# Blocks 0 and 1 of a gated linear attention in front of two MoE layers: the fourth head pair placed by products instead of a shift

## The chip, the cores and the metric

One core of a Trainium2 chip runs the whole program in one launch. The metric is the device time of one execution in microseconds (us); lower is better. The engines are PE (TensorE, matmuls), DVE (VectorE), ACT (ScalarE), POOL (GpSimd) and SP (SyncE, which issues the DMAs). Each engine works through its own instructions in order, and semaphores order the engines among each other.

## The reference

```python
# q, k, v, alpha: [4 batches, 8 heads, 768 steps, 48]
for t in range(S):
    state = alpha[:, :, t, :, None] * state + einsum('bhd,bhe->bhde', k[:, :, t], v[:, :, t])
    y[:, :, t] = einsum('bhd,bhde->bhe', q[:, :, t], state)
x = y.transpose(0, 2, 1, 3).reshape(3072, 384)          # heads side by side
x = ((x @ w_a) * (x @ w_b)) @ w_out                      # 384 -> 1536 -> 384
h = x @ w_in                                             # 384 -> 2048 -> 384
out = (max(h, 0) + alpha2 * min(h, 0)) @ w_out2
```

## The kernel before, in words

The 3072 tokens are cut into 24 chunks of 128 (one batch each) and 6 blocks of four chunks (512 tokens); `n` is the block, `c` the chunk in it. A chunk's 8 heads lie as 4 pairs: `j` is the pair, `i` the half of the partitions (rows 0 to 47 and 64 to 111), and each head fills 48 of 64 rows. MoE matmuls run in FP32R with every operand split into a high and a low part, three matmuls for each product (lines 699, 700 and 702). The weights arrive as 64-bit floats; `conv` makes high and low parts of them, one unit (128 x 768) in six to eight operations on DVE and ACT, with the low part on PE for the units a0, b0 and o0 (`ON_PE`, lines 308 to 310, tile `cl`). Of a0 and b0, `conv` does the first and the second 384 columns one after the other (`halves`), so that the first half of the output columns is ready early.

**The planner.** The program's order is written out by a small list scheduler, `Graph`. Every operation is added with its engine, an estimated duration in ns, a key, the operations that it waits for and sometimes a ring or pool of buffers. The scheduler walks through estimated time and gives each engine, whenever it is free, the ready operation with the smallest key. Where it leaves PE without work for more than 500 ns, `fill` (line 185, tile `wp`) puts bf16 matmuls of ones there, for 0.7 of the gap. On the chip the order is fixed and only the semaphores decide when something runs.

**The steps of the first MoE.** `SEGMENTS` lists them: four steps of block 0 with the units 0 and 1, four of block 1 with the same units, then both blocks with the units 2 and 3, and so on. A step is one tile of 128 hidden columns: an `up` with `a` and one with `b` (9 matmuls each into a PSUM bank of two, `ps_mm`), the product on DVE, its split (ACT, DVE), and two steps later a `down` of 9 matmuls. The ups are chained (`up_before`), so no step of block 1 comes ahead of block 0's four, and none of block 0's unit 2 ahead of block 1's four.

**A chunk.** `scan_r`, `recip`, `scan_a` and `mul` on DVE (lines 402 to 417) scale k and q by running products of alpha. PE transposes k (`kps`, line 453), ACT copies it (`ks`). `pe_a` makes the products of k and q, DVE masks them (`As`). Then

- blocks 1 to 5 work in halves of 64 steps, with tiles of 64 x 64: `pe_a` at line 481, `pe_cross` (`intra` at line 558 for one half of each head, the two states at line 581), `mid` (the state z1 in the middle, DVE), `pe_own` (the other `intra`, then `inter` at line 565 with Z for the first half and z1 for the second). `A` and `y` share one pair of PSUM banks (`pring`), so a chunk's `pe_a` waits until the chunk before has left `y`.
- block 0 has no state before it and works in whole chunks: `pe_a` at line 471, the state at line 528, `pe_y` at lines 544 and 548.

`y` holds four tiles of heads, and the first MoE reads three (`KT`), with 16 free rows (`GR`) beside each head's 48. The two heads of the fourth tile go into these gaps. In block 0 this is done by products with `vg`, a second layout of v that comes from memory with zeros in place (line 548). In block 1 (`moved`), ACT copies the fourth tile out (`ev_3`) and three matmuls with shifted identities add it to the other three (`pe_m`, line 611). In blocks 2 to 5, DMAs move it. `split_h` (ACT, line 657) and `split_l` (DVE, line 661) make the high and low part `x` that the MoE reads.

```python
for h, z in ((0, Z[:, c]), (1, s["z1"])):          # the end of pe_own before
    for j in range(NJ):
        for i in range(2):
            inter(j, i, h, z, h == 1 and j > 1)
```

Of the kernel before, what the change touches and what calls it, by code (L numbers as in the profile page):

```python
# [11 lines left out]
F32 = mybir.dt.float32  # L12
BF16 = mybir.dt.bfloat16
F32R = mybir.dt.float32r
# [7 lines left out]
P = 128  # L22
# [117 lines left out]
def body(tc, akq, v, vg, w_a, w_b, w_o1, w_in, w_o2, beta, out):  # L140
# [13 lines left out]
    with ExitStack() as ctx:  # L154
# [12 lines left out]
        mask = const.tile([P, P], F32, name="mask")  # L167
# [10 lines left out]
        def fill(t0, t1):  # L178
# [13 lines left out]
        nc.gpsimd.affine_select(  # L192
            out=mask, in_=mask, pattern=[[1, P]], compare_op=ALU.is_ge, fill=0.0,
            base=0, channel_multiplier=-1,
        )
# [4 lines left out]
        shift = gpool.tile([P, KT + 1, P], F32, name="shift", tag="x2")  # L200
        nc.gpsimd.memset(shift, 0.0)
        for t in range(KT):
            for i in range(2):
                nc.gpsimd.tensor_copy(
                    out=shift[:, t, 64 * i + D : 64 * i + 64],
                    in_=eye[:, 64 * i + GR * t : 64 * i + GR * (t + 1)],
                )
# [16 lines left out]
        def conv(src, tag, name, key, wait, sink, early=15000, on_pe=False, halves=None):  # L224

            b = {}
            tags = (halves[0], tag) if halves else (tag, tag)
            nt = halves[1] if halves else 1  # L230

            def load():
                b["raw"] = wpool.tile([P, UC], I64, name=f"r{name}", tag=tags[0])
                nc.sync.dma_start(b["raw"], src)

            ld = G.add("SP", 2100, load, key - early, wait, 4000)
            free = cring.take()
            last, highs = [], []
            for n in range(2 if halves else 1):
                N = 2 if halves else 1  # L240
                part = lambda x, n=n: x.rearrange("p (t n f) -> p t n f", t=nt, n=N)[:, :, n, :]
                word = lambda k, dt, part=part: part(b["raw"].bitcast(dt)[:, k::2])
                c1 = lambda part=part: part(b["c1"])
                c2 = lambda part=part: part(b["c2"])
                hi = lambda part=part: part(b["r"][:, 0:UC])
                lo = lambda part=part: part(b["r"][:, UC : 2 * UC])

                def magnitude(n=n, c1=c1, word=word):
                    if n == 0:
                        b["c1"] = cpool.tile([P, UC], F32, name="c1", tag="c1")  # L250
                        b["c2"] = cpool.tile([P, UC], F32, name="c2", tag="c2")


                    nc.scalar.activation(out=c1(), in_=word(1, F32), func=ACTF.Abs, scale=2.0**-112)

                def sign(c2=c2, word=word):
                    nc.vector.tensor_scalar(out=c2().bitcast(U32), in0=word(1, U32),
                                            scalar1=0x80000000, scalar2=None, op0=ALU.bitwise_and)

                def main(c1=c1, c2=c2):  # L260
                    x = c1().bitcast(U32)
                    nc.vector.scalar_tensor_tensor(out=x, in0=x, scalar=3, in1=c2().bitcast(U32),
                                                   op0=ALU.logical_shift_left, op1=ALU.bitwise_or)

                def power(c1=c1, c2=c2):
                    nc.vector.tensor_scalar(out=c2().bitcast(U32), in0=c1().bitcast(U32),
                                            scalar1=0xFF800000, scalar2=None, op0=ALU.bitwise_and)

                def rest(c2=c2, word=word):
                    o = c2()  # L270
                    nc.vector.scalar_tensor_tensor(out=o, in0=word(0, U32), scalar=2.0**-52,
                                                   in1=c2(), op0=ALU.mult, op1=ALU.mult)

                def high(n=n, c1=c1, hi=hi):
                    if n == 0:
                        b["r"] = wpool.tile([P, 2 * UC], F32R, name=f"w{name}", tag=tag)
                    nc.scalar.copy(hi(), c1())

                def sub(c1=c1, hi=hi):
                    nc.vector.tensor_tensor(out=c1(), in0=c1(), in1=hi().bitcast(F32), op=ALU.subtract)  # L280

                def low(c1=c1, c2=c2, lo=lo):
                    nc.vector.tensor_tensor(out=lo(), in0=c1(), in1=c2(), op=ALU.add)
                    sink(b["r"])

                d = lambda t: t // N + 40
                m = G.add("ACT", d(910), magnitude, key, [ld, *(free if n == 0 else ())], after=last)
                x = G.add("DVE", d(550), sign, key, [m])
                x = G.add("DVE", d(930), main, key, [x])
                x = G.add("DVE", d(550), power, key, [x])  # L290
                x = G.add("DVE", d(930), rest, key, [x])
                x = G.add("ACT", d(830), high, key, [x], after=highs)
# [729 lines left out]
```

## Time and profile before

| | |
|---|---|
| median of 3 runs (lowest, highest) | 967.24 us (966.16, 967.24) |
| the profiled execution: its own time, its span | 966.85 us, 965.2 us |
| PE, busy share of the span | 99% |
| DVE, ACT | 62%, 26% |
| filler matmuls `wp`, line 185 | 125, in the first tenth of the span |
| mean granted TensorE clock | 0.999 |

The span runs from the first to the last instruction; 1.65 us of the execution's time lie around it. A busy PE is not PE at its peak: matmuls overlap, and a row of the timeline gives start and length of a run of them, where the length includes the last one's way through the array, so that the distance to the next row's start is what the run costs. In these rows a float32 product counts as two instructions (16 for 8 products of the code).

### The profile page before, as it was taken

The numbers are of one execution on the slowest core, as the hardware profiler recorded it, in microseconds if no ns is written. First come the engines' busy times: TensorE is split into PE (matmuls) and PEld (weight loads), VectorE is DVE, ScalarE is ACT, GpSimd is POOL, SyncE is SP. The second block draws the span as 40 slices with busy tenths as digits, with TensorE's granted clock in tenths as the row PEclk, the third lists the DMA queues.
The fourth block names the chain that finished last, engine by engine and source line by source line (L and its number), as shares of the span: only waits on it lengthen the run. The fifth ranks groups of instructions, "written<-read, shape, count | busy, mean of one in ns | idle before, by whom it ended". The sixth has DMA issues, their size and how long they took to land.

```text
span 965.2 us, 15549 instructions
## 1 busy us (share of the span) xinstructions
PE 952.7 (99%) x6667; PEld 770.4 (80%) x6667; DVE 600.4 (62%) x887; ACT 253.9 (26%) x422; POOL 4.4 (0%) x18
## 2 busy tenths in 40 slices
PE   6999999999999999999999999999999999999998
PEld 5778888778877887887788888888888888888886
DVE  7999888578668868865332254555555545545554
ACT  2444443233333333332221211111111111111111
POOL 1000000000000000000000000000000000000000
PEclk9999999999999999999999999999999999999999
DMA  8971000145456545742065550010100200200000
GB/s 317 407 287 51 12 1 12 45 145 180 150 179 204 206 167 191 240 153 79 25 210 197 196 196 1 27 72 1 65 33 1 89 10 0 99 1 1 33 1 33
DMA packets 31076, 104.09 MB, mean 108 GB/s; under 512 B 3488, under 2 KB 4256, under 8 KB 31008
## 3 DMA queue, kind: packets, MB, share of 16 engines
q1 hardware_dynamic: 30864, 102.97, 30.2%
q8 instruction: 52, 0.85, 0.4%
q10 hardware_dynamic: 144, 0.13, 0.0%
q14 instruction: 16, 0.13, 0.0%
HBM read 74.78 MB, written 26.74 MB: 105 GB/s over the span
## 4 chain that ended last, share of the span: by engine, by line
PE 99%; DVE 0%; DMA 0%; ACT 0%; issue 0%; DVEq 0%; ACTq 0%
PE acc L699 12%; PE acc L702 12%; PE acc L700 12%; PE pi L699 7%; PE pi L702 7%; PE pi L700 7%; PE pb L699 5%; PE pa L699 5%; PE pa L700 5%; PE pb L700 5%; PE pb L702 5%; PE pa L702 5%; PE wp L185 2%; PE y L558 2%; PE kps L453 1%; PE A L481 1%
## 5 line engine op out<-in xcount | busy, mean ns | idle before, releaser
L722 ACT CAST gh<-ng 128x512 fp32r<-128x512 f32 x96 | 59.6, 621 | 328.6 <-DVE ng L935 275.0
L931 DVE TENSOR_SCALAR ng<-pi,betaT 128x512 f32<-128x512 f32 x96 | 72.1, 751 | 106.7 <-PE pi L702 105.8
L726 DVE TENSOR_TENSOR gl<-ng,gh 128x512 fp32r<-128x512 f32 x96 | 66.3, 691 | 79.9 <-ACT gh L722 79.9
L699 PE MATMUL pi<-x,v 128*128 128x512 f32 x288 | 113.3, 393 | 0.0
L700 PE MATMUL acc<-gh,v 128*128 128x512 f32 x288 | 113.1, 393 | 0.0
L702 PE MATMUL acc<-gl,v 128*128 128x512 f32 x288 | 112.9, 392 | 0.0
L700 PE MATMUL pi<-x,v 128*128 128x512 f32 x288 | 112.7, 391 | 0.0
L699 PE MATMUL acc<-gh,v 128*128 128x512 f32 x288 | 112.1, 389 | 0.0
L829 DVE TENSOR_TENSOR a_sb<-a_sb,pb 128x512 f32<-128x512 f32 x72 | 49.4, 686 | 96.5 <-PE pb L702 96.4
L699 PE MATMUL pa<-x,wa 128*128 128x512 f32 x216 | 86.7, 401 | 0.0
L699 PE MATMUL pb<-x,wb 128*128 128x512 f32 x216 | 86.6, 401 | 0.0
L699 PE MATMUL acc<-gh,wo 128*128 128x512 f32 x216 | 86.6, 401 | 0.0
L702 PE MATMUL acc<-gl,wo 128*128 128x512 f32 x216 | 84.9, 393 | 0.0
L700 PE MATMUL pa<-x,wa 128*128 128x512 f32 x216 | 84.7, 392 | 0.0
L700 PE MATMUL pb<-x,wb 128*128 128x512 f32 x216 | 84.6, 392 | 0.0
L700 PE MATMUL acc<-gh,wo 128*128 128x512 f32 x216 | 84.6, 392 | 0.0
L826 ACT COPY a_sb<-pa 128x512 f32<-128x512 f32 x72 | 42.2, 587 | 151.0 <-PE pa L702 151.0
L702 PE MATMUL pi<-x,v 128*128 128x512 f32 x288 | 81.5, 391 | 0.0
L722 ACT CAST gh<-a_sb 128x512 fp32r<-128x512 f32 x72 | 44.8, 622 | 102.6 <-DVE a_sb L829 102.6
L935 DVE SCALAR_TENSOR_TENSOR ng<-pi,ng 128x512 f32<-128x512 f32 x96 | 66.4, 691 | 3.1
L699 PEld LDWEIGHTS pi<-x,v 128*128 128x128 f32 x288 | 54.1, 188 | 13.7 <-DVE ng L935 2.1
L699 PEld LDWEIGHTS acc<-gh,v 128*128 128x128 f32 x288 | 54.0, 188 | 12.3
(120 smaller groups left out, 1426.5 us busy)
## 6 DMA issues: line engine op xcount, KB each, us to landing
kq<-in_akq SPq DMA_DIRECT2D x24, 512.0 KB, 3.8
w2d<-ws SPq DMA_DIRECT2D x16, 768.0 KB, 3.5
v<-w2d SPq DMA_DIRECT2D x16, 768.0 KB, 5.4
x2d<-x SPq DMA_DIRECT2D x18, 512.0 KB, 3.3
x<-x2d SPq DMA_DIRECT2D x6, 1536.0 KB, 6.9
ra<-in_akq SPq DMA_DIRECT2D x24, 258.5 KB, 3.5
v<-in_v SPq DMA_DIRECT2D x24, 256.0 KB, 4.4
rs<-in_w_in SPq DMA_DIRECT2D x8, 768.0 KB, 5.5
```

The costliest lines, as they stand in the source:

```text
L185: nc.tensor.matmul(wp, warm[:, 0:P], warm, start=True, stop=True)
L453: nc.tensor.transpose(s["kps"][:, j, :], kT()[:, j, :], ident)
L558: nc.tensor.matmul(y_of(k, half(p), part_of(h)), s["v"][part_of(h), 2 * j + i, :], s["As"][part_of(h), i, j, :], start=first, stop=False, ...
L699: nc.tensor.matmul(o, lh, rh, start=first and n == 0, stop=False)
L700: nc.tensor.matmul(o, ll, rh, start=False, stop=False)
L702: nc.tensor.matmul(o, lh, rl, start=False, stop=last and n == len(pairs) - 1)
L722: nc.scalar.copy(gq[idx][0], src())
L726: nc.vector.tensor_tensor(out=gl, in0=src(), in1=gh.bitcast(F32), op=ALU.subtract)
L826: nc.scalar.copy(b["a"], ba["t"])
L829: nc.vector.tensor_tensor(out=b["a"], in0=b["a"], in1=bb["t"], op=ALU.mult)
L931: nc.vector.tensor_scalar(out=b["n"], in0=bh["t"], scalar1=0.0, scalar2=betaT[:, i : i + 1], op0=ALU.min, op1=ALU.mult)
L935: nc.vector.scalar_tensor_tensor(out=b["n"], in0=bh["t"], scalar=0.0, in1=b["n"], op0=ALU.max, op1=ALU.add)
```

## The change

It touches blocks 0 and 1, the planner's keys, and two orders inside `pe_cross` and `pe_own` of all blocks.

1. `vg`, its loads, the shifted identities, `ev_3` and `pe_m` go. A zeroed tile `gaps` is kept, and ACT spreads into its 16-column gaps the fourth pair's v (`gather_v`), the middle state z1 and, in block 1, Z (`gather_z`). PE multiplies with these: `intra_moved` in `pe_cross` and `pe_own`, and `pe_pair` after `pe_own`. `intra` and `inter` leave the fourth tile's heads out in blocks 0 and 1.
2. Block 0 takes the path in halves: `pe_a` with 64 x 64 tiles, one masking operation instead of two, z1 by a copy on ACT, the second state inside `pe_own`. Odd and even chunks have their own `ks`, `As` and PSUM banks. For chunks 0 to 2 the low part of `x` is made by PE (`less`) and copied by ACT (`ev_l`) instead of subtracted on DVE.
3. a0 and b0 are converted whole, with a key of -50000 that puts their load and their operations behind block 0 and ahead of block 1. The estimate for the low part on PE falls from 1600 to 1000 ns.
4. In the first segment an `up` is issued as three pieces of three matmuls and a `down` as three pieces.
5. The keys of block 1's chunks lie 8000 apart instead of 9500 and begin earlier; masking, z1 and the splits of block 1 go ahead of everything but block 0 (`chain_early`). The chunks of blocks 2 to 5 get earlier keys too.
6. In all blocks `pe_own` takes the z1 products of `i = 0` first, then its `intra`, then the z1 products of `i = 1`, then those with Z. `pe_cross` goes through the states with the halves of the chunk outside and `i` inside.

```diff
-        shift = gpool.tile([P, KT + 1, P], F32, name="shift", tag="x2")
...
+        gaps = wpool.tile([P, 4, KT, 2, 64], F32, name="gaps", tag=f"w{3 * NU1 - 1}")
+        other = wpool.tile([P, 2 * UC], F32, name="other", tag=f"w{3 * NU1 - 2}")
+        nc.gpsimd.memset(gaps, 0.0)
...
+                                   due[x] - 18000 if u or nm == "o" else -50000, (), sink,
+                                   on_pe=x in ON_PE)
...
-            key = block_at[n] - (BC - c) * 9500 - 6000 if n else c * 1000 - 100000
+            key = block_at[n] - (BC - c) * 12000 - 14000
+            if first:
+                key = c * 1000 - 100000 if start else block_at[1] - (BC - c) * 8000 - 16000
+            odd = start and c % 2
+            chain_early = 100000 if n == 1 else 0
...
+            def intra_moved(k, h):
+                for p in range(2):
+                    nc.tensor.matmul(y_of(k, half(p), part_of(h)), gaps[part_of(h), c % 2, k, p, :],
+                                     s["As"][part_of(h), 1, 2 + p, :], start=False, stop=False,
+                                     skip_group_check=True)
...
+            def state_of(h, j):
+                for i in range(2):
+                    nc.tensor.matmul(dS_of(h)[half(i), j // 2, j % 2, :], s["ks"][part_of(h), j, half(i)],
+                                     s["v"][part_of(h), 2 * j + i, 0:D], start=False, ...
+            def pe_cross():
...
+                for j in range(NJ):
+                    for h in range(2):
+                        intra(j, 1 - h, h, j < 2)
+                if first:
+                    for k in range(KT):
+                        intra_moved(k, 1 - k // 2)
+                for j in range(NJ):
+                    state_of(0, j)
+                    if not (start or end):
+                        state_of(1, j)
...
+            def pe_own():
+                for j in range(NJ):
+                    inter(j, 0, 1, False)
+                for j in range(NJ):
+                    for i in range(2):
+                        intra(j, i, i, False)
+                if first:
+                    for k in range(KT):
+                        intra_moved(k, k // 2)
+                for j in range(NJ):
+                    inter(j, 1, 1, j > 1)
+                if start:
+                    for j in range(NJ):
+                        state_of(1, j)
+                    return
+                for j in range(NJ):
+                    for i in range(2):
+                        inter(j, i, 0, j > 1)
+            def spread(to, src):
+                nc.scalar.copy(to[:, :, :, D:], src.rearrange("p j (t r) -> p t j r", r=GR))
...
+            def pe_pair():
+                for h in range(1 if start else 0, 2):
+                    for k in range(KT):
+                        for p in range(2):
+                            nc.tensor.matmul(y_of(k, half(p), part_of(h)), gaps[:, 2 + h, k, p, :],
+                                             qT()[:, 2 + p, part_of(h)], start=False, stop=True, ...
+            def less():
+                for x, y in two(0):
+                    nc.tensor.matmul(y, minus, x, start=False, stop=True, skip_group_check=True)
+            def ev_l():
+                for x, y in two(1):
+                    nc.scalar.copy(x, y)
...
-            if moved:
-                def ev_3(): ...
-                def pe_m(): ...
```

## Rows read from the trace of the kernel before

**Rows 1.** The page: the chain that ended last, by engine.
```profile
PE 99%; DVE 0%; DMA 0%; ACT 0%; issue 0%; DVEq 0%; ACTq 0%
```

**Rows 2.** Filler of line 185 by stretch: PE busy (x), weight loads, clock, DMA share, GB/s.
```profile
8.00:35.00 27.00, 7.04 (x47) 5.01 (x47) 1.00 0.98 372
35.00:90.00 55.00, 10.06 (x78) 7.03 (x78) 1.00 0.65 247
```

**Rows 3.** All engines: PE, PEld, DVE, ACT, POOL busy, clock, DMA share, GB/s.
```profile
8.00:35.00 27.00, 27.00 (x317) 21.91 (x321) 26.05 (x44) 9.40 (x25) 0.00 (x0) 1.00 0.98 372
```

**Rows 4.** PE's timeline, block 0's last chunk to the first ups: start, length, work.
```profile
26.03 0.88 PE L544 MATMUL y<-As,v 128*64 128x128 f32 x12
...
29.18 0.91 PE L308 MATMUL cl<-c,plus 128*128 128x384 f32 x2
...
35.35 0.51 PE L699 MATMUL pa<-x,wa 128*128 128x512 f32 x1
...
39.61 0.81 PE L308 MATMUL cl<-c,plus 128*128 128x384 f32 x2
...
41.17 0.46 PE L558 MATMUL y<-As,v 64*64 64x64 f32 x16
```

**Rows 5.** PE's timeline, block 1's last chunk to the first step of block 1.
```profile
75.65 0.60 PE L453 MATMUL kps<-plus,kq 128*128 128x128 f32 x4
...
76.80 0.50 PE L699 MATMUL pb<-x,wb 128*128 128x512 f32 x1
...
81.13 0.46 PE L558 MATMUL y<-As,v 64*64 64x64 f32 x16
81.42 0.63 PE L581 MATMUL y<-v,ks 64*64 64x48 f32 x32
81.98 0.61 PE L185 MATMUL wp<-ones 128*128 128x256 bf16 x4
...
84.60 0.46 PE L558 MATMUL y<-As,v 64*64 64x64 f32 x16
84.88 0.41 PE L565 MATMUL y<-kq,Z 48*48 48x64 f32 x16
85.11 0.40 PE L565 MATMUL y<-kq,As 48*48 48x64 f32 x16
85.44 1.38 PE L185 MATMUL wp<-ones 128*128 128x256 bf16 x11
86.66 0.83 PE L611 MATMUL y<-shift 128*128 128x128 f32 x6
87.33 2.13 PE L185 MATMUL wp<-ones 128*128 128x256 bf16 x18
89.21 0.48 PE L699 MATMUL pa<-x,wa 128*128 128x512 f32 x1
```

**Rows 6.** DVE by line and shape up to 90 us: count, busy us, mean ns.
```profile
L262 DVE SCALAR_TENSOR_TENSOR c<-c,c 128x768 uint32<-128x768 uint32 x6 | 5.6, 950 | 0.0
L492 DVE TENSOR_TENSOR As<-A,mask 128x512 f32<-128x512 f32 x8 | 5.5, 682 | 0.7 <-PE A L471 0.7
L266 DVE TENSOR_SCALAR c<-c 128x768 uint32<-128x768 uint32 x6 | 3.2, 552 | 0.0
```

**Rows 7.** DVE's timeline: the scans of block 0's first and second chunk, a split.
```profile
3.78 1.26 DVE L402 TENSOR_TENSOR_SCAN ra<-ra,ones 128x516 f32<-128x516 f32 x1 [3.78 <-DMA ra<-in_akq]
...
7.77 1.23 DVE L402 TENSOR_TENSOR_SCAN ra<-ra,ones 128x516 f32<-128x516 f32 x1
...
28.24 0.60 DVE L661 TENSOR_TENSOR x<-y,x 128x256 fp32r<-128x256 f32 x2
```

**Rows 8.** ACT by line and shape up to 90 us.
```profile
L607 ACT COPY shift<-y 128x128 f32<-128x128 f32 x4 | 1.1, 274 | 1.7 <-PE y L565 1.7
```

**Rows 9.** PE's timeline, the states of a chunk of block 5, one half only.
```profile
452.34 0.63 PE L581 MATMUL y<-v,ks 64*64 64x48 f32 x16
452.90 0.50 PE L699 MATMUL pa<-x,wa 128*128 128x512 f32 x1
```

More of the change, by code (lines that the diff above doesn't have):

```diff
@@ new lines, in high, with sub, low @@
+            def high():
+                b["r"] = wpool.tile([P, 2 * UC], F32R, name=f"w{name}", tag=tag)
+                nc.scalar.copy(hi(), b["c1"])
+            def sub():
+                nc.vector.tensor_tensor(out=b["c1"], in0=b["c1"], in1=hi().bitcast(F32), op=ALU.subtract)
+            def low():
+                nc.vector.tensor_tensor(out=lo(), in0=b["c1"], in1=b["c2"], op=ALU.add)
+                sink(b["r"])
+            ld = G.add("SP", 2100, load, key - early, wait, 4000)
+            x = G.add("ACT", 950, magnitude, key, [ld, *cring.take()])
@@ L397, in chunk @@
             lq = A("SP", 1400, load_kq, lwait, 13800, 3000, [la])
-            lv = A("SP", 1250 if start else 720, load_v, vring.take(), 12000, 3000)
+            vwait, vhold = (vring.take(), vring.last()) if spare is None else ([lq], lhold)
+            lv = A("SP", 720, load_v, vwait, 12000, 3000)
             def scan_r():
@@ new lines, in chunk @@
+            if start:
+                (b0, w0, h0), (b1, w1, h1) = (bank(0), bank(KT)) if c % 2 else (bank(1), bank(2))
+                ybanks, w = (b0, b1), [*w0, *w1]
+            else:
+                w, h0, h1 = pring.take(), pring.last(), []
+            gv = A("ACT", 220, gather_v, [lv, *vgring.take()]) if first else None
+            pc = A("PE", 850, pe_cross, [a0, ks, lv, gv, *w])
+            kring.use(pc)
+            z1 = A("ACT" if start else "DVE", 360, mid, [pc, zs], chain_early)
@@ new lines, in chunk @@
+            own = py = A("PE", 850, pe_own, [z1, zs, q1])
+            kring.use(py)
+            if first:
+                gw = gring1.take()
+                x = [A("ACT", 220, lambda: gather_z(1), [z1, *gw])]
+                if not start:
+                    x.append(A("ACT", 220, lambda: gather_z(0), [zs, *gw]))
+                py = A("PE", 500, pe_pair, [own, *x])
+                gring1.use(py)
+                vgring.use(own)
+                o5 = loads[3 * NU1 - 1]
+                py.users.append(o5)
+                o5.need += 1
@@ L746, in down, with f @@
                     wait += accfree.pop()
-            op = G.add("PE", 9 * MM, f, key, [*deps, *wait],
-                       after=[chain.get(acc)])
+            op = None
+            for part in ([[e] for e in range(KT)] if fine else [range(KT)]):
+                def f(part=part):
+                    if first and 0 in part:
+                        accs[acc] = [ps_acc.tile([P, MB], F32, name=f"acc{e}", tag=f"acc{e}")
+                                     for e in range(KT)]
+                    wh, wl = units[w]
+                    g = gq[idx]
+                    for e in part:
+                        es = slice(e * P, (e + 1) * P)
+                        mms(accs[acc][e], products([((wh[:, o, es], wl[:, o, es]), g)]), range(3), first, last)
+                op = G.add("PE", 3 * len(part) * MM, f, key, () if op else [*deps, *wait],
+                           after=[op or chain.get(acc)])
             chain[acc] = op
```

470 lines of the change are left out of this document (194 added, 276 removed).

## The prediction, made before the changed kernel ran

> **What bounds the kernel now.** I read the page first, then the chain of waits, then PE's timeline of the first 90 us beside DVE's. The chain is PE for 99% of the span [rows 1], and from 8 us on PE has no gap [rows 3], so a microsecond of PE work, real or filler, is a microsecond of the span. The filler tells where PE had nothing real to do: 47 matmuls before 35 us, 78 between 35 and 90, which are all 125 that the table of the page counts [rows 2]. Their lengths sum to 17.1 us; a run's length reaches over the next row's start (1.38 us against 1.22 in rows 5), so I take 15 us of the span as filler. The last run ends where the first step of block 1 starts, at 89.2 us [rows 5]. From there on the span is 876 us of nothing but work.
>
> So two questions decide. How much earlier than 89.2 us can block 1's first step start? And does PE get more to do after it? Before it, PE does 89.2 - 8.0 - 15 = 66.2 us of real work.
>
> **What sets the start.** Until 35 us it is DVE: 26.05 us busy of 27 [rows 3]. Afterwards it is a chain: `A` and `y` share one pair of banks, so block 1's chunks follow each other, and the last takes from 75.65 to 89.21, 13.6 us, in which its own PE work is short and PE fills with filler [rows 5].
>
> **The change, part by part.**
>
> *DVE in block 0.* A chunk's four operations take 7.77 - 3.78 = 4.0 us [rows 7], four chunks 16.0. Masking falls from two operations of 0.68 to one [rows 6]: 4 x 0.68 = 2.7 stay. Three low parts of x at 0.6 [rows 7] go to PE and ACT. a0 and b0, whole, are two operations of 0.95 and two of 0.55 each [rows 6]: 6.0 us for both. From 3.8 us on that is 24.7 us, so DVE is through at 28.5. Then come a high part on ACT, which I set at 0.8 us by the DVE operations of the same shape [rows 6], and four low parts on PE at 41.17 - 39.61 = 1.56 us [rows 4], 6.2 us, of which the first two can start while b0 is still on DVE: the first up at about 34.5 us, against 35.35 [rows 4]. That is little earlier, but all four low parts are then done; before, two of the four (3.1 us) came after the first up.
>
> *PE in block 0.* Before, a chunk is 29.18 - 26.03 = 3.15 us [rows 4] and about 0.5 for the transposes. For the new one I need the price of 64 x 64 products. Where consecutive products change between the two row halves, 8 `intra` take 0.29 us, 16 states 0.56, 8 `inter` 0.23 [rows 5]: 0.03 to 0.035 each. Where all lie in one row half, 8 states take as long as 16 did, 0.56 us [rows 9]: twice the price. By these: transposes and `pe_a` as in block 1, 1.15; `pe_cross` with 4 `intra` in turn and 2 in one half (0.28), `intra_moved` with four in one half and two beside them (0.28), 8 states in one half (0.56), 1.12; `pe_own` with 4 + 2 `inter` in one half (0.34), `intra` and `intra_moved` again 0.56, 8 states 0.56, 1.46; `pe_pair` 6 products of 128 rows and 64 columns, for which 6 of double the moving columns give at most 0.88 [rows 4], 0.4; `less` 0.17, by nine matmuls of 512 columns in 2.1 us [rows 4]. Sum 4.3, so +0.65 a chunk, +2.6 for four, and 0.5 for one more change of shape a chunk (0.1 each, below): 3.1 us.
>
> *PE in block 1.* Before: 1.15 + 0.85 + 0.84 + 0.67 (`pe_m`) = 3.5 us a chunk [rows 5]. New: 1.15; `pe_cross` 0.28 + 0.28 + 0.56 = 1.12; `pe_own` 0.34 + 0.56 + 0.22 = 1.12; `pe_pair` 12 products, 0.8 (bounds: 0.4, by the price of a small product, and 1.8, by 0.88 for six). Sum 4.2: +0.7, for four chunks 2.8 us. The copy of 0.27 on ACT [rows 8] becomes three: `pe_cross` now waits for `gather_v`, `pe_pair` for `gather_z`, where `pe_m` waited for `ev_3`. Behind a waiting one on PE stand MoE pieces and all else; `gather_v` needs only v, which lies there early, so I take 0; uncovered, it is 4 x 0.27 = 1.1 us.
>
> *The start of block 1's steps.* By real work alone: 8.0 + 66.2 + 3.1 + 2.8 = 80.1 us. From the other end: first up 34.5, eight ups and four downs at 2.13 (two take 39.61 - 35.35 [rows 4]) 25.6, block 1 without what runs before the first up 15.6, o0's two low parts 3.1: 78.8. Filler on top: a1, b1 and o0 each need 3.0 us of DVE, a1 and b1 two operations of 0.95 more [rows 6], and DVE has first two chunks of block 1 and the products of two steps to do, so PE runs dry once around 45 us; and the planner now sets the low part on PE at 1.0 us where it takes 1.56, so some filler will stand where none is needed. I take 3 us (bounds 0 and 9, what lies between 80.1 and 89.2). Start at 82.5, so 6.7 us are gained. The pieces of three, the earlier keys and the places ahead of the rest are what lets the chunk's chain run in under 13 us; by themselves they add no work on PE. Pieces can change how often PE goes from one shape to another; a change costs 0.1 us (8 `inter` take 0.33 us before filler, 0.23 before more `inter` [rows 5]): ten more would be 1.0 us, inside the 3.
>
> *Blocks 2 to 5.* Here only the order changes. In `pe_own`, 4 products in the lower row half now stand ahead, and 4 in the upper one behind, where before the halves took turns. Eight products at 0.058 instead of 0.029: +0.23 us a chunk, 16 chunks, **+3.7 us** on an engine without a gap. Bounds: nothing, if PE starts the other half's products past a waiting one; 0.28 (by rows 9's states), 4.5 us. The states in `pe_cross` go by pairs of one half; four in a row still use all four tiles, so I take 0; at rows 9's price throughout it would be 0.56 x 12 = 6.7. `pe_own` also begins with z1 now, so that nothing of it hides a late `mid`: at most one operation of 0.7 us on DVE a chunk, but a planned one, so 0.
>
> [...]
>
> *What is hidden.* ACT gets per chunk of block 0 some 1.3 us more (9.4 of 27 us busy [rows 3]); it has room, and the links are in the chain above. POOL clears a larger tile at the start and loses six small copies: it is done before the first `gather_v`. SP loses four loads of `vg`, and the later chunks of block 0 keep v in slots of their own, so that their loads wait for nothing; the DMA engines are 0.98 busy until 35 us [rows 3], so a0 and b0 ahead of the rest delay the others by their 1.5 MB at 372 GB/s, 4 us, which are due only after 28 us. The slots of `gaps` and `other` are freed later, so o5's and b5's loads wait on SP, with the later loads queued behind; they are first used in the fifth segment, so 0. Earlier keys of blocks 2 to 5: no filler stands there that they could remove.
>
> **Sum**, against the profiled execution (966.85 us, span 965.2): -6.7 + 3.7 = -3.0, so a span of 962.2 and a time of 963.9 us. That execution stands 0.4 us below the median shown.
>
> **Rivals.**
> - *The row halves fill each other.* If PE works past a run in one half, the 3.7 us fall away: 960.2 us. For it: four tiles do work at once in rows 5. Against it: rows 9. [...] 18%.
> - *PE never runs dry* after the first up: start at 79.5, 9.7 gained, 3.7 lost: 960.9. Against it: DVE's 26 of 27 us. 10%.
> - *The chunk's chain keeps its pace (slower).* The new chunk has `pe_pair` and its copy in place of `pe_m` and its copy, as many links, and more PE work. If it still takes 13.6 us [rows 5], four from 34.5 end at 88.9: 0.3 gained, 3.7 lost, 970.3 us. It decides from 12.8 us a chunk (start at 85.5), where gain and loss are equal. For it: the in-order queues have as many hops as before. Against it: the pieces of 0.7 instead of 2.1 us and the first places. 18%.
> - *They cancel*: start at 84.5 to 86, or the states by pairs cost a part of their bound: 966 to 968. 18%. This includes that the change gives DVE time which PE's new work takes back.
>
> **The numbers.** The forecast has 36%, its own range is 961.5 to 966.3. A measurement of this kernel tells 0.2%, 1.9 us, from no change. Faster: most of the forecast (0.29), the first two rivals (0.28): 0.57. Same: the rest of the forecast and the cancelling: 0.25. Slower: 0.18. The range of 8 in 10 reaches from 957.5 (both faster rivals in part together) to 970.5.
>
> **What would show it.** First step of block 1 at 82.5 us; filler down from 17 us to about 6; the first up near 34.5 with all four low parts ahead of it. `pe_own` in blocks 2 to 5 at 0.93 us instead of 0.70 up to its last product: if it stays, the first rival holds. `pe_pair` at 0.8 us in block 1. The forecast is wrong if filler stays above 10 us, or if work other than these terms appears after block 1's first step.

## The result, and the profile after

The changed kernel takes 975.98 us (975.34 to 976.51), the one before 966.7: 1.0096 times as long, 95% interval 1.0079 to 1.0114. Forecast were 963.9 us, so 3 us less; it is 9.3 us more, and above the prediction's range of 8 in 10, which ends at 970.5. The profiled execution of the changed kernel took 976.24 us, its span is 974.5. Sums of PE work below are taken from one product's start to the next one's, since lengths overlap (a run of 0.92 us from 90.51 on reaches past the next start at 91.36).

The end of block 1, on PE's timeline of the changed kernel (start, length, line, work), answers to [rows 5]:

```profile
90.51 0.92 PE L579 MATMUL y<-kq,gaps 128*64 128x64 f32 x24
91.36 0.83 PE L185 MATMUL wp<-ones 128*128 128x256 bf16 x6
...
94.11 2.22 PE L702 MATMUL pa<-x,wa 128*128 128x512 f32 x9
```

Block 1's first step starts at 94.11, and one of four downs of the first segment (2.1 us), which all stood ahead of it before, is still to do. Counted with it the step stands at 96.2: 7.0 us later than 89.21, not 6.7 earlier. (In other runs up to two of the four downs are still to do there; the text says where their 2.1 us each are added.) The other 2.4 us come from blocks 2 to 5, where the products `inter` (line 506) take 12.28 instead of 8.94 us and `intra` (line 490) 8.04 instead of 9.01.

Most of the loss is made before the first up. PE's timeline of the changed kernel there answers to [rows 4]:

```profile
14.13 0.66 PE L437 MATMUL kps<-plus,kq 128*128 128x128 f32 x4
...
19.94 0.98 PE L515 MATMUL y<-v,other 64*64 64x48 f32 x14 [1.63 <-issue]
...
23.81 1.11 PE L437 MATMUL kps<-plus,in 128*128 128x128 f32 x4
...
30.17 0.66 PE L437 MATMUL kps<-plus,in 128*128 128x128 f32 x4
...
34.52 0.49 PE L658 MATMUL y<-x,minus 128*128 128x256 f32 x2
...
44.68 2.31 PE L702 MATMUL pa<-x,wa 128*128 128x512 f32 x9
```

Three things are to be seen. Up to 19.94 PE does nothing for 1.63 us, and the bracket names no semaphore but "issue". From then to about 30 us the same work takes 1.7 times as long: four transposes 1.11 instead of 0.66 us. And the first up starts at 44.68 instead of 35.35 us, 9.3 us late. Of these, 3.1 are the two low parts that stood behind it before, so 6.2 us are lost there; that 9.3 is also the whole loss is chance. All engines by stretch (columns as in [rows 3]):

```profile
8.00:35.00 27.00, 25.25 (x529) 21.07 (x529) 18.31 (x23) 10.51 (x31) 0.00 (x0) 0.81 0.81 311
16.00:20.00 4.00, 2.37 (x71) 1.89 (x62) 3.90 (x6) 0.76 (x3) 0.00 (x0) 0.98 0.96 331
20.00:24.00 4.00, 4.00 (x69) 3.70 (x69) 0.60 (x2) 2.20 (x6) 0.00 (x0) 0.50 0.42 152
24.00:28.00 4.00, 4.00 (x55) 3.13 (x54) 1.04 (x2) 2.19 (x6) 0.00 (x0) 0.50 0.24 61
28.00:32.00 4.00, 4.00 (x116) 3.66 (x116) 3.07 (x5) 1.76 (x6) 0.00 (x0) 0.74 1.04 413
```

The granted clock is 0.50 right after the pause, the lower of the two values in the trace's records (1.00 and 0.50); the pace with it, 1.11 us for four transposes, is called half pace below. DVE, 26.05 of 27 us busy before [rows 3], is down to 18.31, with 6.37 us idle in one piece before it masks the third chunk's products of k and q, which PE makes from 25.69 to 26.82: it waits for PE now (the profile names ACT's `x`, line 650, as what came last; ACT makes it at 26.50, behind a copy of what PE transposed). PE issues 529 matmuls where it issued 317.

Filler by stretch, answering to [rows 2]:

```profile
8.00:35.00 27.00, 5.56 (x27) 3.30 (x28) 0.81 0.81 311
35.00:90.00 55.00, 7.42 (x55) 4.57 (x53) 1.00 0.64 237
90.00:95.00 5.00, 0.83 (x6) 0.50 (x6) 1.00 0.47 159
```

13.8 us in length, 12.0 of the span. The prediction's sum had 3, its list of signs about 6 in length; "the forecast is wrong if filler stays above 10 us" came true.

### The profile page after: what moved, and what is told of

It is laid out like the page before. It is cut to its first block, busy times and chain, and to the rows that moved or that the text cites. A ratio compares the mean times of both kernels' runs of the same rounds, so it can differ in the third digit from the quotient of the medians.

```text
span 974.5 us, 16302 instructions
## 1 busy us (share of the span) xinstructions
PE 960.3 (99%) x7058; PEld 776.7 (80%) x7058; DVE 596.3 (61%) x865; ACT 259.0 (27%) x439; POOL 3.7 (0%) x13
## 4 chain that ended last, share of the span: by engine, by line
PE 98%; DVE 0%; DMA 0%; issue 0%; ACT 0%; DVEq 0%; ACTq 0%
PE acc L702 36%; PE pi L702 20%; PE pa L702 16%; PE pb L702 16%; PE y L490 2%; PE A L460 2%; PE y L506 2%; PE y L515 1%; PE kps L437 1%; PE wp L185 1%; PE y L579 1%; PE cl L284 0%; PE y L496 0%; PE cl L286 0%; DMA ra<-in_akq 0%
## 5 line engine op out<-in xcount | busy, mean ns | idle before, releaser
L702 PE MATMUL pi<-x,v 128*128 128x512 f32 x864 | 211.6, 392 | 0.0
L702 PEld LDWEIGHTS pi<-x,v 128*128 128x128 f32 x864 | 161.9, 188 | 37.2 <-DVE ng L944 2.1
L702 PE MATMUL acc<-gh,v 128*128 128x512 f32 x576 | 178.3, 391 | 0.0
L702 PEld LDWEIGHTS pb<-x,wb 128*128 128x128 f32 x648 | 120.1, 188 | 26.3
L702 PEld LDWEIGHTS pa<-x,wa 128*128 128x128 f32 x648 | 119.8, 188 | 26.3
L940 DVE TENSOR_SCALAR ng<-pi,betaT 128x512 f32<-128x512 f32 x96 | 72.1, 751 | 106.5 <-PE pi L702 105.6
L702 PEld LDWEIGHTS acc<-gh,v 128*128 128x128 f32 x576 | 108.1, 188 | 24.2
L702 PEld LDWEIGHTS acc<-gh,wo 128*128 128x128 f32 x432 | 79.8, 188 | 17.7
L729 ACT CAST gh<-a_sb 128x512 fp32r<-128x512 f32 x72 | 44.7, 621 | 109.5 <-DVE a_sb L838 104.6
L702 PEld LDWEIGHTS acc<-gl,v 128*128 128x128 f32 x288 | 54.1, 188 | 11.3
L733 DVE TENSOR_TENSOR gl<-a_sb,gh 128x512 fp32r<-128x512 f32 x72 | 49.3, 684 | 17.4 <-ACT gh L729 17.4
L702 PEld LDWEIGHTS acc<-gl,wo 128*128 128x128 f32 x216 | 40.6, 188 | 8.7
```

The source lines that it names most:

```text
L702: nc.tensor.matmul(o, *seq[n], start=first and n == 0, stop=last and n == len(seq) - 1)
L729: nc.scalar.copy(gq[idx][0], src())
L733: nc.vector.tensor_tensor(out=gl, in0=src(), in1=gh.bitcast(F32), op=ALU.subtract)
L940: nc.vector.tensor_scalar(out=b["n"], in0=bh["t"], scalar1=0.0, scalar2=betaT[:, i : i + 1], op0=ALU.min, op1=ALU.mult)
```

## The experiments

Three causes were in question: block 0's halves starve PE (it pauses on their short products, by the theory for want of instructions, and then works at half pace); estimates that are too short put filler where real work waits; the order, the pairs of block 1 or the first places cost the time. Theories and rivals are numbered anew in each group of runs; each expectation says what its number means. Each time stands beside its ratio to the kernel before, measured with it, and the 95% interval. The median of the kernel before lies between 966.5 and 966.9 us in the groups, so differences between runs of different groups carry some tenths of a us. The edits are given in short, not as the code's own lines.

**The order, the estimates, the filler, one by one, in the changed kernel.**

```diff
 e2: def pe_own(): if not first: intra, then inter by turns of i   (order of before)
 e3: G.add("PE", 1000 -> 1560, add ...); pe_cross 850 -> 1080; pe_own 850 -> 1310/1050/930; pe_pair 500 -> 500/850; transposes 480 -> 530; pe_a 600 -> 630
 e4: def fill(t0, t1): return
```

> Blocks 2 to 5 get the old order in pe_own back, the rest is the changed kernel. Theory 1 (a run in one row half leaves the other half idle): inter falls from 24.0 to 17.5 ns an instruction in 16 chunks, 3.3 us less, so 972.6 us against 976.0. Rival (the halves fill each other and the loss lies in blocks 0 and 1 alone): 976, no difference.

974.7 us, 1.0079 (1.0065 to 1.0092); `inter` is back at 8.94 us.

> The planner's estimates for PE's operations are set to what the trace of the changed kernel shows (low part on PE 1.56 us, pe_cross 1.08, pe_own 1.05 and 1.31, pe_pair 0.85, transposes 0.53); nothing else is changed. Theory 1 (PE is late against the plan, and filler stands where its work is already due): planned filler falls from 21 to 7 us after 9 us of planned time, the time falls by 4 to 8 us, to 968 to 972. Rival 3 (block 0's chain of short operations feeds PE late, filler lies in waits): below 1 us either way, 975 to 977.

974.3 us, 1.0088 (1.0073 to 1.0102), with 6.1 us of filler instead of 12.0: neither the 968 to 972 of the theory nor the rival's 975 to 977. With the downs still to do added, block 1's first step stands at 90.9, 5.3 us earlier than in the changed kernel. But in block 2 PE then waits twice for DVE, 0.88 and 1.42 us, and behind that the granted clock is 0.50 for 3.4 us, so that 1.7 us are left of the 5.3:

```profile
233.03 0.36 PE L506 MATMUL y<-kq,As 48*48 48x64 f32 x5 [1.42 <-DVE As L544]
```

> The changed kernel without any filler matmul. [...] Rival 3 (filler lies in waits): the same time at full clock, 975 to 977, and over 977 where the clock falls.

974.2 us, 1.0079 (1.0066 to 1.0092). None by itself explains 9.3 us: the three are 1.3 to 1.8 us under the changed kernel, and all their intervals overlap with its own. The first up stays at 48.2, 43.4 and 45.7 us (48.2 is from an execution of 977.45 us, 2.8 above that run's median). Without filler PE has one gap of 1.0 us, at 11 us, and then next to none up to 35 us, and is late all the same. Its timeline there:

```profile
12.76 1.11 PE L438 MATMUL kps<-plus,kq 128*128 128x128 f32 x4
...
22.57 1.11 PE L438 MATMUL kps<-plus,in 128*128 128x128 f32 x4
...
28.21 1.11 PE L438 MATMUL kps<-plus,in 128*128 128x128 f32 x4
```

The lengths are those of the half pace throughout, where the changed kernel was at full pace behind its first run of filler (0.66 at 14.13). So the filler that it saves, 12 us, buys 1.8 at most.

**Block 0 in whole chunks.** Masks, states and y as before the change, the low parts of x on DVE; the rest of the change stays. Then also the old order (e6), then also honest estimates (e8).

```diff
 e5: if start: pe_a into two banks, two masked products, pe_d, pe_y; gather_v kept; no halves, no less/ev_l
 e6: + old order of pe_own in blocks 2 to 5
 e8: + PE 1000 -> 1560 (low part), 1080, 1050, 850 in block 1; 830, 700 in blocks 2 to 5
```

> Block 0 goes back to whole chunks (two masked operations, dS and y in single products of 128 rows, z of the chunk kept from dS, low part of x on DVE); a0 and b0 stay whole and ahead, block 1 keeps the new form, blocks 2 to 5 the new order. Theory 1 (the halves of block 0: twice as many short products, PE runs out of instructions at its 220th matmul, and then works at half pace): no pause, 4 transposes at 0.60 us instead of 1.11 throughout 20 to 30 us, the first up at 36 to 38 us instead of 44.7, the time 967 to 970 us. Rival 2 (what is late is the whole conversion of a0 and b0 with its four low parts ahead of the first up): the first up stays at 42 us or later, the time is above 972. Rival 3 (the pairs of block 1 and the order cost the time): the first up is early, but block 1's first step stays behind 92 us and the time above 973.

972.4 us, 1.0059 (1.0044 to 1.0074). PE's timeline:

```profile
20.26 0.60 PE L439 MATMUL kps<-plus,in 128*128 128x128 f32 x4
...
25.38 0.62 PE L439 MATMUL kps<-plus,in 128*128 128x128 f32 x4
...
36.97 2.51 PE L758 MATMUL pa<-x,wa 128*128 128x512 f32 x9
```

Pause and half pace are gone, and the first up comes at 36.97 as expected. The time does not: 3.6 us were gained, not 6 to 9. Block 1's first step is at 86.81 with two downs still to do, so at 91.0 where the changed kernel has 96.2: part of the 7.7 us is lost again between the two.

> As the run before it, and blocks 2 to 5 with the old order of the own products. If the order is worth what the products show (512 inter at 24.0 instead of 17.5 ns an instruction, less what intra gets back: 2.4 us), it takes 2 to 3 us less than the run before it: by theory 1 965 to 967 us, by rival 2 970, by rival 3 971. If the order costs nothing, both have the same time.

969.5 us, 1.0033 (1.0020 to 1.0045): the order is worth 2.9 us here. The time itself is near the 970 of rival 2, not the 965 to 967 of theory 1.

> As the second run of this call, and the durations that the planner is given for PE as the trace shows them: low part 1.56 us instead of 1.0, cross of block 1 1.08, own 1.05, pair 0.85 (cross 0.83 and own 0.70 in the later blocks). If filler placed by too short durations costs time, filler falls by 3 us or more and the time by 1 to 3 us against the second run: 963 to 965 by theory 1. If filler stands only where PE would wait anyway, the time is the same within 0.5 us.

968.4 us, 1.0016 (1.0006 to 1.0025): 1.2 us for the estimates, not the 963 to 965 us expected; the filler hardly falls, 13.4 instead of 14.1 us.

**Is it the pause?** The changed kernel was first profiled a second time, unchanged (e1): 976.35 us, a single execution. What had been expected: without the pause the first up comes some 5 us earlier. The pause is there again, but what follows it is not:

```profile
19.74 0.61 PE L515 MATMUL y<-v,other 64*64 64x48 f32 x14 [1.68 <-issue]
...
22.09 0.66 PE L437 MATMUL kps<-plus,in 128*128 128x128 f32 x4
...
25.93 0.65 PE L437 MATMUL kps<-plus,in 128*128 128x128 f32 x4
...
31.47 0.50 PE L579 MATMUL y<-in,gaps 128*64 128x64 f32 x9 [2.81 <-issue]
...
44.63 2.31 PE L702 MATMUL pa<-x,wa 128*128 128x512 f32 x9
```

The granted clock stays at 1.00 until 32.8 us and is 0.50 for 3.4 us only then. The last chunk's transposes come at 25.93 instead of 30.17. Then PE pauses again, for 2.81 us, and the first up is where it was, at 44.63 against 44.68; block 1's first step is at 94.05 against 94.11. So the half pace is not a loss on top of the pauses: at full pace PE reaches the next pause sooner.

In e7 and e11 wide products stand ahead of the places where PE pauses, and nothing else is changed.

```diff
 pe_cross of block 0:
+    if start and c == 1:          # e11: c in (1, 2), 1 + c times
+        for _ in range(2):
+            nc.tensor.matmul(y0, ident, ones[:, 0:512], start=True, stop=True)
```

> The changed kernel with one addition: two products of 128 rows and 512 fp32 columns stand before block 0's second cross, some 30 matmuls ahead of the place where PE pauses; their result is overwritten. They cost about 1.7 us of PE. Theory 1 (pause, then half pace): PE is still busy with them while the instructions land, so the pause of 1.63 us goes or shrinks below 0.5; if the pace holds as well, the first up comes at 41 to 42 us and the time is 972 to 974. Rival 2 (the chain behind the masked products, not pause and pace): the first up is 45 to 46.5 us and the time 976 to 978.

977.5 us, 1.0110 (1.0095 to 1.0125): the first pause went as expected, the time did not fall. Time and first up are those that rival 2 expected, but there is a second pause:

```profile
17.91 1.88 PE L530 MATMUL y<-ones,plus 128*128 128x512 f32 x4
...
22.57 0.66 PE L437 MATMUL kps<-plus,in 128*128 128x128 f32 x4
...
26.41 0.63 PE L437 MATMUL kps<-plus,in 128*128 128x128 f32 x4
...
31.77 0.34 PE L515 MATMUL y<-in,ks 64*64 64x48 f32 x1 [2.93 <-issue]
...
46.32 2.31 PE L707 MATMUL pa<-x,wa 128*128 128x512 f32 x9
```

The pace stays full for 9 us more, and then PE pauses again, longer, 255 matmuls after the place of the first pause: the same place as in e1. So this run doesn't tell the two apart; the next one does.

> The changed kernel with two wide products before block 0's second cross, as before, and three more before the third cross, behind the 348th matmul (the run with the first two alone paused 2.93 us at its 476th). If PE pauses when it has worked off 128 matmuls faster than the next 16 KB of instructions come (4.5 to 6.6 us from the 348th on), the second pause goes below 0.5 us too, the pace stays full from 13 us on (4 transposes 0.60 to 0.66 us), and the first up is at 43.5 to 44.5 us, of which 4.6 are the wide products; the time is 974 to 976. If the pause comes at a place and not by the rate, it stays, and the first up is at 48 us or later.

975.1 us, 1.0089 (1.0074 to 1.0104):

```profile
25.23 2.79 PE L530 MATMUL y<-ones,plus 128*128 128x512 f32 x6
...
28.97 0.66 PE L437 MATMUL kps<-plus,in 128*128 128x128 f32 x4
...
31.74 0.43 PE L515 MATMUL y<-in,ks 64*64 64x48 f32 x7 [0.48 <-issue]
...
43.82 2.31 PE L707 MATMUL pa<-x,wa 128*128 128x512 f32 x9
```

Pauses below 0.5 us, full pace, first up at 43.82, 2.5 us before e7's although three wide products more stand ahead of it: as expected of a pause that comes by the rate, and not of one at a place or of a chain that sets the first up. Of the 43.82, 1.88 + 2.79 = 4.7 are the wide products: without them it would be 39.1, an estimate for a PE at full pace with pauses below 0.5 us, which no execution of the changed kernel shows. By it pauses and half pace are 44.7 - 39.1 = 5.6 us of the 9.3 by which the first up is late; of the other 3.7, 3.1 are the two low parts more that now stand ahead of it. Pauses and half pace are the larger part.

**Only the halves undone**, with the buffers and banks that odd and even chunks had to themselves; low parts of x on PE and ACT as in the change (e16); then honest estimates as well (e17); then the old order (e15).

```diff
 e16: as e5, but: if start and c < BC - 1: xl = less on PE, ev_l on ACT
 e17: + estimates 1560, 1080, 1050, 850 (830, 930 in blocks 2 to 5)
 e15: + old order of pe_own in blocks 2 to 5 (estimate 700)
```

> The changed kernel with whole chunks in block 0 as the only difference: low parts of x of the first three chunks on PE and ACT, new order in blocks 2 to 5, the short estimates, pairs and keys all stay. If the halves are the main cause (more short products, PE out of instructions, half pace), 7 to 9 us go: first up at 36 to 39 us, 967 to 969 us, which with the order (2.9) and the estimates (1.2) taken off comes to the 963.9 of the run before. If they cost only what the run with whole chunks showed (3.6), it stays at 972 to 973.

970.7 us, 1.0043 (1.0026 to 1.0060): the halves cost 5.3 us, between the two expectations.

> The changed kernel with whole chunks in block 0 and honest estimates for PE (low part 1.56 us, cross of block 1 1.08, own 1.05, pair 0.85; later blocks cross 0.83 and own 0.93); the new order of blocks 2 to 5 stays. If the order is worth its 2.9 us everywhere, 966.5 to 967 us, and the estimates are worth some 4 us with low parts on PE (filler 8.5 instead of 11.6 us, block 1's first step at 82.6 instead of 86.1). If the estimates stay at 1.2, it is 969.5.

968.7 us, 1.0020 (1.0010 to 1.0030), between the two again. Block 1's first step starts at 82.2 instead of 86.1 (two downs still to do in both), but only 2.0 us of that reach the end. PE's timeline and DVE's in block 2:

```profile
226.12 0.46 PE L514 MATMUL y<-As,v 64*64 64x64 f32 x16 [0.89 <-DVE As L476]
...
228.45 0.36 PE L530 MATMUL y<-kq,As 48*48 48x64 f32 x5 [1.42 <-DVE As L568]
```
```profile
225.98 0.68 DVE L857 TENSOR_TENSOR x<-part,x 128x512 fp32r<-128x512 f32 x1
226.58 0.95 DVE L257 SCALAR_TENSOR_TENSOR c<-rs,c 128x768 f32<-128x768 uint32 x1
227.45 0.68 DVE L834 TENSOR_TENSOR part<-part,acc 128x512 f32<-128x512 f32 x1
228.04 0.35 DVE L568 TENSOR_TENSOR As<-y,Z 128x192 f32<-128x192 f32 x1
```

PE, further ahead, waits 2.3 us for DVE; the second wait is for `mid`, behind which nothing of `pe_own` is left to hide it.

> The changed kernel with whole chunks in block 0, old order in blocks 2 to 5, honest estimates (968.4 us before), and the low parts of x of block 0's first three chunks on PE and ACT again, as in the change. If DVE in block 0 sets the first up here too, it takes 1 to 2.2 us off: 966 to 967.4. Against the second run of this call, which has block 1 in the old form, the pairs then cost 2.5 us or more; if the pairs cost nothing, both runs are within 1 us.

963.9 us, 0.9969 (0.9956 to 0.9981), under the 966 to 967.4 expected: against e8 the low parts on PE are worth 4.5 us here, not 1 to 2.2. No such wait; block 1's first step and the first of two downs still to do stand at

```profile
82.58 2.32 PE L768 MATMUL pa<-x,wa 128*128 128x512 f32 x9
...
86.79 0.62 PE L768 MATMUL acc<-gh,wo 128*128 128x512 f32 x2
```

What is left of the change, low parts on PE, pairs, pieces, places and keys, thus saves 2.9 us against the kernel before, which has its step at 89.2 where this one has 86.7, the two downs added. The old order is worth 4.8 us from e17 to e15, of which 2.3 are the waits.

**The planning alone, in the kernel before.** Pieces of three (e9); pieces, block 1's keys and first places (e10); these and the keys of blocks 2 to 5 (e13). Pieces and the low parts of x of block 0 on PE (e12); e13 with these low parts (e14).

```diff
 e9:  up(..., fine=s == 0), down1(..., fine=s == 0)
 e10: + n == 1: key = block_at[1] - (BC - c) * 8000 - 16000; chain_early for As, mid, split_h, split_l
 e13: + key = block_at[n] - (BC - c) * 12000 - 14000 for n > 1
 e12: e9 + if start and c < BC - 1: xl = less on PE, ev_l on ACT
 e14: e13 + the same
```

> The kernel before with one part of the change alone: the ups and downs of the first segment (block 0, two units) are issued in pieces of three matmuls instead of nine. If the short issues by themselves let block 1's operations in between them sooner, the first step of block 1 comes 1 to 2 us before 89.2 and the time is 965 to 966 us; if they only change how often PE goes from one shape to another, 967 to 968; without either 966.6.

965.7 us, 0.9990 (0.9980 to 0.9999), step at 87.9 with all four downs done.

> As the run before it, and block 1's keys and first places as in the change (chunks keyed 8 us apart, its masked product, mid, high and low part of x ahead of all else on their engines); its products stay in the old form with the moving matmuls. Theory (filler in block 1 is there because of the chain from chunk to chunk): first places shorten the chain, filler between 45 and 90 us falls from some 10 us to 7 and the time to 963 to 965. Rival (DVE and the PE order set it, not the places): the time is 966 to 969, and filler only moves.

972.6 us, 1.0067 (1.0049 to 1.0085). The filler between 35 and 90 us falls from the 10.06 us of the kernel before to 2.71 us of length, better than expected, and the step starts at 81.69, or at 85.8 with the two downs still to do; yet the time is 6.9 us above e9's. PE's timeline in the profiled execution (975.54 us, the slowest of four):

```profile
81.69 2.31 PE L705 MATMUL pa<-x,wa 128*128 128x512 f32 x9
...
225.45 0.46 PE L561 MATMUL y<-As,v 64*64 64x64 f32 x16 [1.36 <-DVE As L499]
...
227.78 0.70 PE L561 MATMUL y<-As,v 64*64 64x64 f32 x16 [1.42 <-DVE As L590]
...
320.14 0.46 PE L561 MATMUL y<-As,v 64*64 64x64 f32 x16 [2.42 <-DVE As L499]
```

The 3.4 us gained at the start against the kernel before are given back and more, 140 to 240 us later, at masked products that DVE does too late: the waits shown are 5.2 us, and behind them the granted clock is 0.50 for 6.8 us from 226.9.

> The pieces and first places of the run before (972.6 us), and now the changed kernel's keys for the chunks of blocks 2 to 5 as well (12 us a chunk and 14 ahead, instead of 9.5 and 6); all products and the conversion of a0 and b0 in the old form. Theory (those chunks came too late for a PE that is 4 us ahead: waits of 1.4, 1.4, 2.4 us and more before masked products): the waits go, block 1's first step stays near 82 us, and the time is 964 to 966. Against the changed kernel with whole chunks, old order and honest estimates (968.4) it then leaves 2.5 to 4 us for the pairs of block 1. Rival (PE ahead waits for DVE wherever the chunks are put): 969 or more.

967.0 us, 1.0001 (0.9989 to 1.0013): the keys take the waits at 320 us away, not those at 225. This median stands between two groups. Five executions took 964.7 to 966.0 us, about the 964 to 966 expected, with a mean granted clock of 0.998 to 1.000; five took 967.9 to 969.0 with 0.995 or 0.996. The profiled one (968.46) is of the second group, and its clock (the number before the last two) falls behind the two waits of 1.36 and 1.42 us:

```profile
226.00:234.00 8.00, 6.58 (x107) 5.41 (x100) 6.41 (x10) 2.08 (x4) 0.00 (x0) 0.57 0.74 204
```

It is 0.50 for 6.8 us from 227.1 on, which costs about 3.4 us by half of that length, an estimate, as much as the two groups are apart. Whether the first group has the waits as well is not known: none of it was profiled.

> The kernel before with the pieces, and in block 0 the low parts of x of the first three chunks on PE and ACT (x's high part taken off y by a product, the rest copied) instead of DVE; block 0 stays in whole chunks, block 1 and the later blocks in the old form. It takes 3 x 0.6 = 1.8 us from DVE, which is busy 26.05 of 27 us in 8 to 35, and gives PE three times 0.35 us where it has 7 us of filler. If DVE sets the first up, it comes 1 to 1.8 us before 35.35, and the time is 1 to 2 us under that of the run with the pieces alone: 964 to 966. If the chain from chunk to chunk sets it, the two more links cost 0 to 1 us and the time is 966 to 968.

963.5 us, 0.9969 (0.9959 to 0.9980), the first up at 33.90, block 1's first step at 85.2 and no waits later: 2.2 us under e9. DVE did set the first up there.

> As the first run of this call, and block 0's first three low parts on PE and ACT, which took 2.2 us off in the old plan. If the gain comes from DVE in block 0 it adds to the planning part: 1 to 2.2 us under the first run, 962 to 964 us. If both remove the same waits, it stays within 0.7 us of the first run.

968.0 us, 1.0011 (1.0001 to 1.0021), neither 1 to 2.2 us under e13 nor within 0.7 of it, with the waits at 227 us in it. It has the two groups too: 965.7 to 967.4 us at 0.999 or 1.000, 968.6 to 969.6 at 0.995 to 0.998. The low parts that gained 2.2 us in e12 gain nothing here. e12 and e15 beat both kernels.

## Why the prediction was wrong

**The failed step** is "DVE is through at 28.5 [...] the first up at about 34.5 us". It took DVE as the bound of block 0 after the change as before, with no wait for PE in it, and added PE's work only as a sum; in the changed kernel DVE's last operation on b0 ends at 36.5. (Nor is 34.5 worked out: 28.5 + 0.8 and two or four low parts give 32.4 or 35.5.) PE's own path shows more: from the first masked product at 13.1 on come four chunks of 4.3 us (less the 1.15 of the first that lie before), four low parts of 1.56 and 1.0 for block 1's first chunk, all in order, so 36.4 us by the prediction's own prices. The estimate without pauses is 39.1, of which 2.0 are filler behind 13.1; the changed kernel comes to 44.7. The 5.6 between are pauses and half pace, which no term of the sum had: every product was priced by rows in which PE was at full pace and without a gap (27.00 of 27 us busy up to 35 us, with 317 matmuls), and nothing was asked about a PE with 529 there.

**The second one** is "I take 3 us" of filler: it is 12.0. The prediction saw that the low part is planned at 1.0 us where it takes 1.56 and still left it within the 3 us. e1, nearly all at full pace, puts the two side by side: up to block 1's first step with the missing down, 96.15 us, it starts at 7.9 (8.0 forecast), has 11.7 us of filler (3 forecast), 4.5 us of pauses (none forecast), and 72.1 us are left for real work: the forecast's 66.2 + 3.1 + 2.8 to the tenth, where some luck is in. So the price of the work was right; filler and pauses were not. Filler costs nearly its length here: e3 has 5.9 us less of it and its step is 5.3 us earlier, though most of that is lost again in block 2.

Without the halves and with honest estimates (e15) the pauses go, but 8.5 us of filler stay and the first up is at 38.3. From there to block 1's first step, the two downs added, are 48.4 us, where the prediction had 48.0 (34.5 to 82.5); in the changed kernel it is 51.5. That e15 takes the 963.9 us that were forecast is chance: it has neither the halves nor the new order that the forecast paid for.

**Point by point.** Work in block 0: 4.3 us a chunk forecast; at full pace, from the last chunk's transposes at 30.17 to the third's `less` at 34.52, one round takes 4.35, and `less` 0.33 more. Work in block 1: +2.8 forecast; the products of e6, new form, are 11.9 us against 9.4, +2.5, `pe_pair` 0.85 at 90.51 where 0.8 was forecast. The order: +3.7 forecast with bounds of 0 and 4.5; PE's products take 2.4 us more (12.28 + 8.04 against 8.94 + 9.01), pairs of runs 1.3 (e2, intervals overlap), 2.9 (e5, e6) and, with a new wait, 4.8 (e17, e15). By form, in blocks 2 to 5, the changed kernel and then e6 (count, busy us, mean ns):

```profile
L506 PE MATMUL y<-kq,As 48*48 48x64 f32 x256 | 13.2, 220 | 0.0
L506 PE MATMUL y<-kq,Z 48*48 48x64 f32 x256 | 9.0, 218 | 0.0
```
```profile
L530 PE MATMUL y<-kq,Z 48*48 48x64 f32 x256 | 6.5, 215 | 0.0
L530 PE MATMUL y<-kq,As 48*48 48x64 f32 x256 | 6.5, 216 | 0.0
```

A single product is as long in both (218 and 220 against 215 and 216 ns); what grows is the time in which any of them runs (13.2 and 9.0 us against 6.5 and 6.5), so fewer run at a time: with `As` 4.3 on average against 8.5, by these sums. That the other row half is idle beside a run in one was the author's estimate from [rows 9]; the sums agree with it and don't show the halves apart. States by pairs: 0 forecast, 8.99 against 8.98 us, right. "`mid`, a planned one, so 0": right in the changed kernel, 1.42 us where PE is ahead (e17). "Earlier keys of blocks 2 to 5", priced at nothing: 5.7 us between the medians of e10 and e13.

**The rivals.** That the halves fill each other and that PE never runs dry fell. The slower one kept the sign, not the mechanism: it wanted 13.6 us a chunk from a first up at 34.5, and four chunks from 44.68 to 96.2 take 12.9 each, hardly over its point of 12.8; what made the kernel slower lies mostly before the first up. That it named the right sign was luck.

Step by step, one run to the next: halves 5.3, estimates 2.0, order 4.8 us, together 12.1 from 976.0 down to 963.9. The steps aren't independent: with the low parts on DVE the estimates were worth 1.2 and the order 2.9, and the low parts on PE themselves 1.7 (e5, e16), 2.2 (e9, e12), 4.5 (e8, e15) or nothing (e13, e14). Why two plans with the same products leave a wait in block 2 or don't (e13, e14, e17 against e12, e15) was not traced further than to the order on DVE.

## What to carry to other kernels

When a change moves the bound from one engine to another, walk the new bound's path in order, from its first release on; a sum of work against the old bound is no start time. Price a run of many short products as a whole; block 0's were not had at the sum of their prices: what one execution lost in a pause of 1.63 us and 10.2 us of half pace behind it, another lost mostly in two pauses of 1.68 and 2.81 us, and their first ups were equally late (44.68 and 44.63 us). Before a start time is compared with that of another plan, count what work still lies behind it. Take a plan's gain at the start for real only where the later stages are shown to keep it.

## What the runs showed of the hardware

**PE's pauses and the fetches of 16 KB.** The changed kernel's profile has 55 fetches of 16 KB on the queue named instruction beside 7058 matmuls, one for about 128. PE stops behind its 221st matmul and goes on at 19.94 us; a fetch runs from 17.36 to 18.44, so it has landed 1.5 us before. In e1 PE stops behind the 221st and again behind the 476th, and goes on at 31.47; in e7 it stops behind the 476th and goes on at 31.77. From the 93rd matmul to the end of the first pause it is 5.7 us in the changed kernel (14.29 to 19.94), from the 348th to the end of the second 6.6 us in e7 (25.13 to 31.77) and in e1 (24.92 to 31.47), about 128 matmuls each; without the pause, block 0's halves go through as many in 3.8 (14.29 to 18.10). The kernel before needs 9 to 12 us for 128 (17.76 to 26.95, 26.95 to 38.92) and never pauses there, and the changed kernel at half pace, with 8.6 (19.94 to 28.49), doesn't either. That PE waits for instructions in the pauses, which come at a limited rate, is the author's reading: the fetch at 18.44 and e11, with 0.48 us where e7 has 2.93, agree with it; no run shows it by itself. A fetch is itself about 1.0 us long (1.08 here); what sets its start, what lies between its landing and PE's next matmul, and whether the data beside it delay it (the DMA engines are 1.03 busy from 12 to 16 us and 0.96 from 16 to 20) was not tested.

**The clock column and the pace.** In e4 PE works from 11 to 35 us with hardly a gap, four transposes take 1.11 us there as at a clock of 0.50 in the changed kernel, and the column of the granted clock shows 1.00 in all of it; the mean clock of that execution is 0.999. The first four transposes at 8 us, 1.09 us long before and after the change, show 1.00 as well. There the lengths tell the pace, not the column: the trace of the changed kernel has no record of the clock before 13.00 us, and the column shows 1.00 from 0 to 12 all the same, so it counts time without a record as 1.00.

**What comes before a fall of the clock.** In the changed kernel the granted clock falls to 0.50 at 19.83 us, at the end of the pause of 1.63 us (18.31 to 19.94), for 10.2 us. In e1 the pause of 1.68 us at the same place is followed by 1.00; there the clock falls at 32.8, behind the second pause of 2.81 us, for 3.4 us. So a pause of 1.6 to 1.7 us is followed by half pace in one of these two executions of the same program and not in the other.
